# Means of the values: earlier loads on 128 partitions, a product on TensorE that adds halves, and value tiles of two blocks

## Chip, cores and metric

One program on one core of a Trainium2 chip. The metric is the device time of one execution in microseconds (us). The engines are TensorE (PE; PEld is its weight load), VectorE (DVE), ScalarE (ACT), GpSimd (POOL) and SyncE (SP, which here only issues DMAs and loads registers). The core has 16 DMA engines, which all queues share.

## The reference, cut to what matters

```python
B, H, S, D = 4, 8, 768, 64;  block, window = 32, 16
k_sum = k.reshape(B, H, 24, 32, D).max(axis=3)
v_sum = v.reshape(B, H, 24, 32, D).mean(axis=3)
scores = concat([where(|i - j| < 16, q @ k.T / 8, -1e9), q @ k_sum.T / 8 + log(32)])
attn   = softmax(scores) @ concat([v, v_sum])
x      = attn as [B * S, H * D]                       # 3072 tokens of 512
e      = argmax(x @ w_gate)                           # one of 8 experts a token
out    = gate * sigmoid(x @ w_output_gate)[e] * (relu(x @ w1[e]) @ w2[e])
```

Attention is local (a band of 16 on each side) with 24 summaries a head: the largest key and the mean value of each 32 tokens. A mixture of experts with one expert a token follows. The change is in how the 24 mean values of each head are made and brought to where the attention product reads them.

## The kernel before

**Stages.** A batch has 768 tokens, which are 6 "tokens tiles" (`tok`) of 128, or 12 blocks of 64. A stage is `(b, tok, g)`: 128 queries and 4 of the 8 heads; there are 48 stages. For a stage, `scores(i)` multiplies queries by the 96 keys of the band and the 24 summaries (120 columns a block; tile `sp`), DVE adds the mask and takes the minimum (`sm`, `mn`), ACT takes the exponential (`pr`), `turn_p(i)` transposes it on TensorE (`pt`, evacuated to `pT`), and `values(i)` multiplies it by the 120 rows of values of that block (`pv`), after which DVE divides (`xs`) and POOL stores 128 tokens to `x_dr`. `scores` is written one stage ahead of `turn_p`, and `values` one behind. `turn_x`, `logits`, `turn_logits` and `route` compute the gates some stages later; the last batch also carries the first expert's weights (`late_work`). The expert products (`hp`, `yp`) follow.

**Loads.** Queries and keys come in thirds of a batch (`raw_q`, `raw_k`), are reordered by a copy (`nat_q`, `nat_k`, mostly on DVE) and transposed (`qtr`, `ktr`). Queries of a third are loaded two thirds ahead, at an even `tok`, and reordered at the next `tok`.

**Values.** `VW` is a ring of 9 tiles of one block each: 120 partitions of 8 heads by 72 columns (64 values, a one, padding). Rows 0 to 47 and 72 to 119 are the band, loaded by `load_vw` in two DMAs a block with runs of 256 bytes; rows 48 to 71 are the 24 means, loaded by `load_vsum` from the DRAM tensor `vs_dr` in runs of 256 bytes, for 9 of a batch's 12 blocks (the other three find a tile of the same batch that has them). The means themselves: `load_vm` brings 4 heads of a batch's values as 96 partitions (4 heads by 24 summaries) of 32 rows; `v_sum` halves them five times on POOL (32 rows to 1), `mean` scales, and a POOL DMA stores 96 rows of 256 bytes to `vs_dr`. The first half of batch 0 is reduced by DVE instead. For batch b + 1 this happens during stages 1 to 7 of batch b.

**What sets the order.** SP's instructions stand as the code writes them; the other engines' order (but POOL's and parts of DVE's in the expert part) is set by a scheduler at build time, which keeps each engine's queue fixed: an instruction that waits holds up all that stand behind it on its engine. So a value load that waits for a ring tile to come free also holds up the query and key loads behind it on SP. SP's loads for token tile `tok + 2` are written at stage `(tok, 0)`.

Of the kernel before, what the change touches and what calls it, by code (L numbers as in the profile page):

```python
# [15 lines left out]
ALU = mybir.AluOpType  # L16
# [15 lines left out]
BUFS = {"sm": 4, "mn": 4, "pr": 4, "pT": 3, "xs": 3, "den": 3, "xT": 2, "ls": 2, "rawk": 3, "rawq": 2, "natk": 2, "natq": 2}  # L32
RAWS = 6
RAWS2 = 10
VR = 9
# [37 lines left out]
C_END = C_SEL + 2 * E  # L73


def constants():
# [22 lines left out]
    c[:, C_SEL:C_SEL + 2 * E] = p[:, None] % 32 == np.arange(2 * E)[None, :]  # L99
    return c  # L100
# [77 lines left out]
def attention(tc, const, sa, sb, st, ps, dr, q, k, v, id_sb, c_sb, wg_sb, x_dr, l_dr, rt, late_work):  # L178
# [24 lines left out]
    vs_dr = dr.tile([B, H, NS, D], F32, name="vs_dr")  # L203
# [21 lines left out]
    def load_vm(b, *os):  # L225
        for o in os:
            t = sa.tile([96, 32 * D], F32, name=f"vm{b}{o}", tag="vm", bufs=2)
            nc.sync.dma_start(t, v[b, 4 * o:4 * o + 4].rearrange("g (n s) d -> (g n) (s d)", n=NS))
            vm[b, o] = t

    vs = {}

    def v_sum(b, o, half):
        t = vm[b, o]
        if (b, o) == (0, 0):
            if half == 0:
                vs[b, o] = sb.tile([96, D], F32, name=f"vs{b}{o}", tag="vs", bufs=2)
            hs = slice(32 * half, 32 * half + 32)
            i = nc.vector.tensor_reduce(out=vs[b, o][:, hs], in_=t.rearrange("p (s d) -> p d s", d=D)[:, hs, :], axis=AX.X,
                                        op=ALU.add)  # L240

            tc.add_manual_dep(i.ins, km["last"].name, mybir.DependencyInfo(mybir.DependencyClass.NoSync,
                                                                           mybir.DependencyReason.SCHED_ONLY))
            if half == 1:
                mean(b, o, vs[b, o])
            return

        n = 16 * D
        if half == 0:
            nc.gpsimd.tensor_tensor(t[:, 0:n], t[:, 0:n], t[:, n:2 * n], ALU.add)  # L250
            return
        while n > D:
            n //= 2
            nc.gpsimd.tensor_tensor(t[:, 0:n], t[:, 0:n], t[:, n:2 * n], ALU.add)
        mean(b, o, t[:, 0:D])

    def mean(b, o, total):
        r2 = sb.tile([96, D], F32, name=f"vm2{b}{o}", tag="vs2", bufs=2)
        if b == 0 and o == 0:
            nc.scalar.activation(r2, total, AF.Copy, scale=1.0 / 32.0)  # L260
        else:
            (nc.gpsimd if b == 0 else nc.vector).tensor_scalar(r2, total, 1.0 / 32.0, None, ALU.mult)
        nc.gpsimd.dma_start(vs_dr[b, 4 * o:4 * o + 4].rearrange("g n d -> (g n) d"), r2)

    def load_vw(b, tok):
        for blk in (2 * tok, 2 * tok + 1):
            t = VW[(NB * b + blk) % VR]
# [6 lines left out]
    def load_vsum(b, tok):  # L274

        for blk in (2 * tok, 2 * tok + 1):
            if blk < VR:
                nc.sync.dma_start(VW[(NB * b + blk) % VR][LW:LW + NS, :, 0:D], vs_dr[b].rearrange("h n d -> n h d"))
# [29 lines left out]
    def k_sum(b):  # L308
        kt = KT[b % 2]
        for hp in range(HP):  # L310
            own = kt[:, hp, PAD:PAD + NB * KW].rearrange("p (i w) -> p i w", w=KW)[:, :, 32:56]
            i = nc.vector.tensor_copy(own, km[b, 0][:, hp, :].unsqueeze(1).to_broadcast([P, NB, NS]))
        km["last"] = i.ins
# [15 lines left out]
    def scores(i):  # L329
# [4 lines left out]
        for x in range(2):  # L334
            for y in range(2):
                li = 2 * tt + y
                blk = 4 * u + li
                nc.tensor.matmul(sp[:, 2 * x + y, 0:W], lhsT=qt[:, 2 * g + x, li, :],  # L338
# [12 lines left out]
    def turn_p(i):  # L351
# [3 lines left out]
        for c in range(4):  # L355
            nc.tensor.transpose(pt[:, c, :], pr[:, c, :], id_sb)  # L356
# [700 lines left out]
```

## Time and profile before

| | |
|---|---|
| Three runs | 539.55, 544.69 (median), 546.93 us |
| Profiled execution | 537.39 us, of which the span of instructions is 535.6 us |
| Granted TensorE clock, mean | 0.978 |
| Busy: PE, PEld, DVE, ACT, POOL | 492.9, 428.5, 387.0, 336.2, 204.1 us |
| First and last `values` product | at 31.46 us and about 195 us |
| DMA | 117.98 MB in 117052 packets, 53787 of them under 512 bytes |

All that follows reads the profiled execution. Its times are microseconds from the span's start. In a timeline row the columns are start, duration, engine, line, operation, tile written <- tiles read, shape and count; what stands in brackets is the idle time of that engine ahead of the row, and what ended it. SPq is SP's DMA queue. In a windows row the columns are the window, its length, busy time (and count) of PE, PEld, DVE, ACT and POOL, the granted TensorE clock, the mean busy share of the 16 DMA engines (it can pass 1 where packets of several queues overlap) and GB/s.

### The profile page before, as it was taken

Reading aid. Unit: us, or ns where it says so; the run is one execution under the profiler, and the core shown is the slowest. Engines: PE = TensorE matmul, PEld = TensorE weight load, DVE = VectorE, ACT = ScalarE, POOL = GpSimd, SP = SyncE. Lnnn points to the kernel's source line nnn. Section 1 sums busy time; section 2 is a strip of 40 time slices with the busy share of each in tenths; the row PEclk is TensorE's granted clock in tenths of the full one; section 3 lists DMA queues with packets and bytes.
Section 4 is the critical chain, followed back from the end, with each engine's and each line's share of the span. In section 5 each row is a group of like instructions: output and inputs, shape, how many; then the busy total and the mean of one; then the engine's idle time right before and its main releaser. Section 6 shows DMA issues by size and latency. Waiting matters only on the chain.

```text
span 535.6 us, 12274 instructions
## 1 busy us (share of the span) xinstructions
PE 492.9 (92%) x3880; PEld 428.5 (80%) x3880; DVE 387.0 (72%) x1238; ACT 336.2 (63%) x753; POOL 204.1 (38%) x231
## 2 busy tenths in 40 slices
PE   5899998789987999999999999999999999999990
PEld 5687887587766798789898998989897887987870
DVE  8877888479958868987666667675667767768660
ACT  4776786487769756554655656565567567558460
POOL 7527157245443432333735071421333421611321
PEclk9789999899999999999999999999999999999996
DMA  8989999899698577595966749486476796696640
GB/s 246 242 207 249 231 247 207 178 222 263 157 196 226 167 236 253 190 193 183 331 205 218 230 166 319 143 284 214 183 264 204 258 304 237 216 311 241 198 159 30
DMA packets 117052, 117.98 MB, mean 220 GB/s; under 512 B 53787, under 2 KB 78651, under 8 KB 116192
## 3 DMA queue, kind: packets, MB, share of 16 engines
q1 hardware_dynamic: 107584, 97.02, 64.5%
q0 software_dynamic: 9376, 19.91, 11.3%
q8 instruction: 36, 0.59, 0.5%
q14 instruction: 56, 0.46, 0.3%
HBM read 106.30 MB, written 13.79 MB: 224 GB/s over the span
## 4 chain that ended last, share of the span: by engine, by line
PE 61%; DMA 17%; DVE 6%; SPq 5%; issue 4%; ACT 3%; POOL 0%; POOLq 0%; ACTq 0%; DVEq 0%
PE hp L846 8%; PE hp L845 8%; PE hp L847 8%; PE yp L945 7%; PE yp L943 7%; PE yp L944 7%; DMA xg<-x_dr,lst_w 5%; PE sp L338 4%; DMA raw_q<-in_q_dram 4%; DMA vw<-vs_dr 3%; PE pv L367 3%; DMA raw_k<-in_k_dram 2%; PE pt L356 2%; PE xp L827 2%; SPq L272 1%
## 5 line engine op out<-in xcount | busy, mean ns | idle before, releaser
L845 PE MATMUL hp<-xhl,w1h 128*128 128x256 f32 x384 | 108.4, 284 | 1.1 <-ACT w2h L815 1.1
L846 PE MATMUL hp<-xhl,w1h 128*128 128x256 f32 x384 | 108.8, 284 | 0.0
L847 PE MATMUL hp<-xhl,w1l 128*128 128x256 f32 x384 | 108.5, 283 | 0.1
L943 PE MATMUL yp<-w2h,hh 128*128 128x512 f32 x216 | 86.5, 401 | 0.3 <-ACT hh L914 0.2
L945 PE MATMUL yp<-w2h,hl 128*128 128x512 f32 x216 | 84.9, 395 | 0.1
L944 PE MATMUL yp<-w2l,hh 128*128 128x512 f32 x216 | 84.9, 393 | 0.0
L794 POOL DMA_INDIRECT xg<-x_dr,lst_w x26 | 30.5, 1173 | 123.5 <-PE xp L827 118.7
L845 PEld LDWEIGHTS hp<-xhl,w1h 128*128 128x128 f32 x384 | 73.2, 191 | 2.9 <-issue 1.5
L846 PEld LDWEIGHTS hp<-xhl,w1h 128*128 128x128 f32 x384 | 73.5, 191 | 2.1 <-DVE xhl L830 0.9
L847 PEld LDWEIGHTS hp<-xhl,w1l 128*128 128x128 f32 x384 | 73.5, 191 | 0.3 <-issue 0.3
L348 ACT ACTIVATE pr<-sm,mn 128x120 f32<-128x120 f32 x192 | 61.5, 386 | 18.3 <-DVE mn L346 17.9
L848 ACT ACTIVATE hh<-hp 128x256 fp32r<-128x256 f32 x96 | 35.2, 380 | 53.4 <-PE hp L847 43.6
L849 DVE SCALAR_TENSOR_TENSOR hl<-hp,hh 128x256 fp32r<-128x256 f32 x96 | 38.8, 419 | 37.6 <-ACT hh L848 22.9
L338 PE MATMUL sp<-kt,qt 128*128 128x120 f32 x384 | 53.6, 287 | 2.2 <-DVE mn L346 0.8
L338 PEld LDWEIGHTS sp<-kt,qt 128*128 128x128 f32 x384 | 48.4, 199 | 5.6 <-issue 2.3
L945 PEld LDWEIGHTS yp<-w2h,hl 128*128 128x128 f32 x216 | 40.4, 188 | 9.8 <-DVE hl L915 1.2
L346 DVE CUSTOM_DVE_ANT_0 sm<-sp,c_sb 128x120 f32<-128x120 f32 x192 | 42.2, 276 | 8.2 <-PE sp L338 5.3
L943 PEld LDWEIGHTS yp<-w2h,hh 128*128 128x128 f32 x216 | 40.7, 188 | 8.6 <-ACT hh L914 0.7
L944 PEld LDWEIGHTS yp<-w2l,hh 128*128 128x128 f32 x216 | 40.7, 188 | 7.9
L356 PE MATMUL pt<-id_sb,pr 128*120 128x128 f32 x192 | 38.7, 288 | 4.6 <-ACT pr L348 1.9
L367 PE MATMUL pv<-vw,pT 120*64 120x65 f32 x768 | 36.3, 231 | 6.8 <-DVE xs L377 2.8
L367 PEld LDWEIGHTS pv<-vw,pT 120*64 120x64 f32 x768 | 28.6, 139 | 16.0 <-issue 7.9
(736 smaller groups left out, 1039.5 us busy)
## 6 DMA issues: line engine op xcount, KB each, us to landing
vw<-in_v_dram SPq DMA_DIRECT2D x88, 96.0 KB
raw_k<-in_k_dram SPq DMA_DIRECT2D x12, 512.0 KB
raw_q<-in_q_dram SPq DMA_DIRECT2D x12, 512.0 KB
vm<-in_v_dram SPq DMA_DIRECT2D x8, 768.0 KB
x_dr<-xs POOLq DMA_DIRECT2D x24, 256.0 KB
vw<-vs_dr SPq DMA_DIRECT2D x36, 48.0 KB
vw<-in_v_dram SPq DMA_DIRECT2D x8, 64.0 KB
xg<-x_dr,lst_w POOLq DMA_INDIRECT x26
```

The costliest lines, as they stand in the source:

```text
L338: nc.tensor.matmul(sp[:, 2 * x + y, 0:W], lhsT=qt[:, 2 * g + x, li, :], rhs=kt[:, 2 * g + x, blk * KW:blk * KW + W], start=True, stop=True)
L346: nc.vector.tensor_tensor_reduce(out=sm[:, c, :], in0=sp[:, c, 0:W], in1=c_sb[:, m:m + W], scale=1.0, scalar=3.0e38, op0=ALU.add, op1=ALU. ...
L348: nc.scalar.activation(pr[:, c, :], sm[:, c, :], AF.Exp, bias=mn[:, c:c + 1], scale=-1.0)
L356: nc.tensor.transpose(pt[:, c, :], pr[:, c, :], id_sb)
L367: nc.tensor.matmul(po[64 * y:64 * y + 64, 2 * x + hh, :], lhsT=pT[:, 2 * x + y, 64 * hh:64 * hh + 64], rhs=VW[(NB * b + 2 * tok + y) % VR] ...
L845: nc.tensor.matmul(hp, lhsT=w_h[:, fs], rhs=self.xh[:, c, :], start=c == 0, stop=False)
L846: nc.tensor.matmul(hp, lhsT=w_h[:, fs], rhs=self.xl[:, c, :], start=False, stop=False)
L847: nc.tensor.matmul(hp, lhsT=w_l[:, fs], rhs=self.xh[:, c, :], start=False, stop=c == NC - 1)
L849: nc.vector.scalar_tensor_tensor(hl[:, j, :], hp, 0.0, hh[:, j, :].bitcast(F32), ALU.max, ALU.subtract)
L943: nc.tensor.matmul(y, lhsT=hh[:, j, tk], rhs=w_h, start=j == 0, stop=False)
L944: nc.tensor.matmul(y, lhsT=hh[:, j, tk], rhs=w_l, start=False, stop=False)
L945: nc.tensor.matmul(y, lhsT=hl[:, j, tk], rhs=w_h, start=False, stop=j == NF - 1)
```

## The change

- **Loads of values for the means** (`load_vm`): three a batch instead of two, each 256 tokens of all 8 heads on 128 partitions (head, 16 tokens) of 16 rows; 4 buffers of 4 KB a partition instead of 2 of 8 KB. From batch 2 on they are issued during the batch before the previous one (`load_ahead`).
- **Sums** (`v_sum`): POOL halves three times (16 rows to 2), in one stage; none for batch 0, and none on DVE.
- **A product** (`v_mean`): TensorE multiplies by a constant of 128 by 64 (`C_MEAN`, 1/32 where head and summary agree), adding up the 2 rows that are left (16 rows for batch 0) and the two partitions of a summary, into 64 rows (8 summaries by 8 heads); ACT copies it to one of three tiles `mean0` to `mean2`, which carry the one and the padding.
- **The store** (`v_store`) writes 64 rows of 288 bytes; `vs_dr` now is [batch, summary, head, 72], so that `load_vsum` reads 2304 bytes in one piece a summary.
- **The ring** has 5 tiles of two blocks (10 blocks) instead of 9 of one. `load_vsum` fills both blocks with one DMA, for 5 of 6 token tiles, and stands one stage later in SP's order. Of the ring's memsets only the ones and 32 rows of one block are left.
- **`natq`** has one buffer instead of two.

```diff
-BUFS = {..., "natk": 2, "natq": 2}
+BUFS = {..., "natk": 2, "natq": 1}
-VR = 9
+VR = 5
...
+    for h, s in np.ndindex(H, 8):
+        c[16 * h + 2 * s:16 * h + 2 * s + 2, C_MEAN + 8 * s + h] = 1.0 / 32.0
...
-        t = sb.tile([W, H, VP], F32, name=f"vw{i}", tag=f"vw{i}", bufs=1)
-        nc.gpsimd.memset(t, 0.0)
-        nc.gpsimd.memset(t[:, :, D:D + 1], 1.0)
+        t = sb.tile([W, 2, H, VP], F32, name=f"vw{i}", tag=f"vw{i}", bufs=1)
+        if i == 0:
+            nc.gpsimd.memset(t[0:32, 0], 0.0)
+        nc.gpsimd.memset(t[:, :, :, D:D + 1], 1.0)
...
+    def load_vm(b, o):
+        t = sa.tile([P, 16 * D], F32, name=f"vm{b}{o}", tag="vm", bufs=4)
+        nc.sync.dma_start(t, v[b, :, 256 * o:256 * o + 256].rearrange("h (x s) d -> h x (s d)", s=16))
+        vm[b, o] = t
+    def v_sum(b, o):
+        t, n = vm[b, o], 16 * D
+        while n > 2 * D:
+            n //= 2
+            nc.gpsimd.tensor_tensor(t[:, 0:n], t[:, 0:n], t[:, n:2 * n], ALU.add)
+    def v_mean(b, o, after=None):
+        t = vm.pop((b, o))
+        mt = ps.tile([64, D], F32, name=f"mt{b}{o}", tag="TR", bufs=PB["TR"])
+        rows = 16 if b == 0 else 2
+        for s in range(rows):
+            i = nc.tensor.matmul(mt, lhsT=c_sb[:, C_MEAN:C_MEAN + 64], rhs=t[:, s * D:(s + 1) * D], start=s == 0,
+                                 stop=s == rows - 1)
+            ...
+        evac("mt", means[o][:, 0:D], mt)
+    def v_store(b, o):
+        nc.gpsimd.dma_start(vs_dr[b, 8 * o:8 * o + 8].rearrange("n h d -> (n h) d"), means[o])
...
+        if tok < VR:
+            t = VW[(TB * b + tok) % VR][LW:LW + NS]
+            nc.sync.dma_start(t.rearrange("n y h d -> n y (h d)"),
+                              vs_dr[b].rearrange("n h d -> n (h d)").unsqueeze(1).to_broadcast([NS, 2, H * VP]))
...
     def load_ahead(b, tok):
+        if tok in (0, 2) and b + 1 < B:
+            load("k", k, b + 1, 1 + tok // 2)
+        if tok == 4 and b + 2 < B:
+            load("k", k, b + 2, 0)
+        if tok in (2, 3, 5) and b + 2 < B:
+            load_vm(b + 2, (2, 3, 5).index(tok))
...
-        if more and u < 2 and s in (1, 3):
-            second.append(lambda: v_sum(b + 1, u, s // 2))
+        if more and i % 12 < 7:
+            o, what = divmod(i % 12, 2)
+            if o < 3:
+                second.append(lambda: (v_mean if what else v_sum)(b + 1, o))
+            if what == 0 and o > 0:
+                second.append(lambda: v_store(b + 1, o - 1))
```

Where this moves instructions. **TensorE at the start**: the stages of batch 0, token tiles 0 to 2 (names end in batch, token tile, g; `mt02` is batch 0, third 2). Before:

```order
L338 MATMUL sp000_306<-kt0_143,qt0_141 128x120 x4
L338 MATMUL sp001_328<-kt0_143,qt0_141 128x120 x4
L356 MATMUL pt000_351<-id_sb_66,pr000_313 120x128
L338 MATMUL sp010_367<-kt0_143,qt0_141 128x120 x4
L356 MATMUL pt000_351<-id_sb_66,pr000_313 120x128 x3
L338 MATMUL sp011_424<-kt0_143,qt0_141 128x120 x4
L356 MATMUL pt001_383<-id_sb_66,pr001_335 120x128 x3
L289 MATMUL qtr010_344<-id_sb_66,nat_q01_290 128x128 x4
```

and now the same place on TensorE:

```order
L339 MATMUL sp000_281<-kt0_143,qt0_141 128x120 x4
L255 MATMUL mt00_297<-vm00_180,c_sb_68 64x64 x16
L255 MATMUL mt01_316<-vm01_182,c_sb_68 64x64 x16
L339 MATMUL sp001_341<-kt0_143,qt0_141 128x120 x4
L358 MATMUL pt000_364<-id_sb_66,pr000_288 120x128 x4
L339 MATMUL sp010_409<-kt0_143,qt0_141 128x120 x4
L291 MATMUL qtr010_357<-id_sb_66,nat_q01_271 128x128 x4
L255 MATMUL mt02_371<-vm02_184,c_sb_68 64x64 x16
```

Two groups of 16 mean products stand between the first two stages' scores, and the third group behind the transposes of the second third's queries, `qtr010`. (TensorE's first `values` product, `pv000`, now stands behind the scores of seven stages; before it stood behind five.)

**SP in batch 1**: around the loads of the queries `raw_q21` and keys `raw_k30`, which the code writes at token tile 4 of batch 1. Before:

```order
L271 DMA vw4_163<-in_v_dram 48x8x64
L272 DMA vw4_163<-in_v_dram 48x8x64
L271 DMA vw5_166<-in_v_dram 48x8x64
L272 DMA vw5_166<-in_v_dram 32x8x64
L209 DMA raw_q21_1480<-in_q_dram 128x8x128
L209 DMA raw_k30_1482<-in_k_dram 128x8x128
L271 DMA vw6_169<-in_v_dram 32x8x64
L272 DMA vw6_169<-in_v_dram 48x8x64
```

and now the same place on SP:

```order
L239 DMA vm31_1387<-in_v_dram 128x1x1024
L272 DMA vw1_154<-in_v_dram 48x8x64
L273 DMA vw1_154<-in_v_dram 48x8x64
L272 DMA vw1_154<-in_v_dram 48x8x64
L273 DMA vw1_154<-in_v_dram 32x8x64
L221 DMA raw_q21_1534<-in_q_dram 128x8x128
L221 DMA raw_k30_1536<-in_k_dram 128x8x128
L272 DMA vw2_156<-in_v_dram 32x8x64
```

The order of the loads is much the same; what differs is when a ring tile is free. The load ahead of `raw_q21` fetches block 11 of batch 1. In the ring of 9 its tile `vw5` was last read for block 2 of that batch (token tile 1); in the ring of 5 pairs its tile `vw1` was last read for token tile 0, one token tile (two stages) earlier. The first expert products and all that follows them on each engine stand as before.

More of the change, by code (lines that the diff above doesn't have):

```diff
@@ L72 @@
 C_SEL = C_PART + 1
-C_END = C_SEL + 2 * E
+C_MEAN = C_SEL + 2 * E
+C_END = C_MEAN + 64
 def constants():
@@ L201, in evac @@
             nc.scalar.activation(dst, src, AF.Copy, scale=1.0 if scale is None else scale)
-    vs_dr = dr.tile([B, H, NS, D], F32, name="vs_dr")
+    vs_dr = dr.tile([B, NS, H, VP], F32, name="vs_dr")
+    means = []
+    for i in range(3):
+        t = sb.tile([64, VP], F32, name=f"mean{i}", tag=f"mean{i}", bufs=1)
+        nc.vector.memset(t[:, D:VP], 0.0)
+        nc.vector.memset(t[:, D:D + 1], 1.0)
+        means.append(t)
     raws, nat = {}, {}
@@ L349, in scores @@
         prs[i] = pr
+        return i_sp
     def turn_p(i):
@@ L478, in attention @@
     load("q", q, 0, 0)
-    load_vm(0, 0, 1)
+    for o in range(3):
+        load_vm(0, o)
     for u in range(3):
@@ L519, in attention @@
     n = len(stages)
-    scores(0)
+    i_sp = scores(0)
+    for o in range(2):
+        v_mean(0, o, i_sp)
+        v_store(0, o)
     for i, (b, tok, g) in enumerate(stages):
@@ L561, in attention @@
             work()
-        turn_p(i)
+        i_pt = turn_p(i)
+        if i == 0:
+            v_mean(0, 2, i_pt)
+            v_store(0, 2)
+            for t in range(3):
+                load_vsum(0, t)
+            for x in range(1, 3):
+                load_vm(1, x)
         second = first[1:] + second
```

76 lines of the change are left out of this document (18 added, 58 removed).

## Prediction, made before the run

> **What bounds the kernel now.** I read the page's head and chain first, then the busy times by stretch, then the waits of the stretch that is worst.
>
> ```profile
> span 535.6 us, 12274 instructions
> PE 61%; DMA 17%; DVE 6%; SPq 5%; issue 4%; ACT 3%; POOL 0%; POOLq 0%; ACTq 0%; DVEq 0%
> ```
>
> TensorE carries 61% of the chain; DMA follows with 17%. The stretches differ, though:
>
> ```profile
> 16.30:31.46 15.16, 13.77 (x76) 11.59 (x77) 10.64 (x46) 10.99 (x31) 6.93 (x8) 0.76 0.88 173
> 31.46:82.00 50.54, 49.11 (x600) 42.69 (x600) 41.52 (x222) 39.77 (x108) 22.52 (x27) 1.00 1.08 247
> 82.00:120.00 38.00, 30.52 (x337) 25.35 (x335) 25.97 (x132) 24.04 (x66) 19.93 (x22) 0.96 0.97 202
> 120.00:150.00 30.00, 27.97 (x337) 22.81 (x335) 26.99 (x153) 20.46 (x54) 14.56 (x17) 1.00 0.88 207
> 150.00:205.00 55.00, 49.05 (x537) 42.25 (x538) 42.16 (x200) 41.45 (x102) 22.04 (x25) 1.00 0.74 199
> 205.00:535.60 330.60, 312.54 (x1925) 275.01 (x1923) 225.61 (x468) 191.47 (x378) 108.37 (x99) 0.98 0.68 223
> ```
>
> From 205 us on the experts' products fill TensorE (312.5 of 330.6 us), and the change moves nothing there. What it can touch are the 189 us between the first scores (16.30) and 205. In 31.46 to 82 TensorE is busy for 49.1 of 50.5 us: nothing that only frees DMA or DVE can gain much there. From 82 to 120 it is busy for 30.5 of 38 us, and to 205 it idles another 8 us. The DMA share is near 1 up to 120 us, but it is a mean of 16 engines, with holes in it. The deepest stall shows how they arise:
>
> ```profile
> 91.01 0.40 SPq L209 DMA_DIRECT2D raw_q<-in_q_dram  x1
> ...
> 100.53 0.69 DVE L220 COPY nat_q<-raw_q 128x1024 f32<-128x1024 f32 x1 [3.61 <-DMA raw_q<-in_q_dram]
> ...
> 102.28 1.14 PE L367 MATMUL pv<-vw,pT 120*64 120x65 f32 x16 [2.80 <-DVE xs L377]
> ...
> 92.00:94.00 2.00, 2.00 (x30) 1.77 (x29) 1.19 (x12) 2.00 (x8) 1.53 (x2) 1.00 0.31 45
> 102.00:104.00 2.00, 1.72 (x24) 1.15 (x24) 0.89 (x3) 0.00 (x0) 1.18 (x2) 0.56 0.50 84
> ```
>
> SP issues the queries' load only at 91.01, with the DMA engines near idle (share 0.31 in 92 to 94); they land 9.5 us later, DVE stands before its copy for 3.61 us, and the division `xs` behind that copy keeps TensorE's product waiting for 2.80 us. The granted clock then falls to 0.56. SP was late because loads into the ring (L271) wait for products that free its tiles:
>
> ```profile
> SPq L271 <- PE pt L356: 7.5, 6, 3.7
> SPq L278 <- DMA vs_dr<-vm: 5.9, 2, 3.3
> ```
>
> **The change part by part.**
>
> *Products for the means.* No such product is in the trace. A call of an f32 product leaves two records, a transpose one. Prices per call from the chain:
>
> ```profile
> 65.52 0.62 PE pv L367 x16
> 62.87 1.78 PE sp L338 x16
> 54.57 0.58 PE pt L356 x4
> ```
>
> A `values` call (64 columns of weights, 65 moving) costs 0.62/8 = 0.078 us, a `scores` call (128 and 120) 1.78/8 = 0.22 us. The new call (64 and 64) is nearest to `values`; but there neighbours go to alternating halves of the columns, and here all add up in one place, so I take twice that, 0.155 us, with 0.078 and 0.22 as ends. Batches 1 to 3 have 18 calls: 18 x 0.155 = **+2.8 us** (1.4 to 4.0) on a TensorE that is nearly full. Batch 0 has 48: 7.4 us (3.7 to 10.6).
>
> *Start.* What lies there now:
>
> ```profile
> L338 PE MATMUL sp<-kt,qt 128*128 128x120 f32 x40 | 7.6, 357 | 1.1 <-ACT qt L201 0.6 <-issue 0.5
> L356 PE MATMUL pt<-id_sb,pr 128*120 128x128 f32 x20 | 4.8, 311 | 0.8 <-ACT pr L348 0.8
> L289 PE MATMUL qtr<-id_sb,nat_q 128*128 128x128 f32 x8 | 1.7, 354 | 0.0
> L289 PE MATMUL ktr<-id_sb,nat_k 128*128 128x128 f32 x8 | 1.7, 354 | 0.0
> ...
> 15.95 3.70 DVE L239 TENSOR_REDUCE vs<-vm 96x32 f32<-96x1024 f32 x2
> 21.95 1.17 DVE L220 COPY nat_q<-raw_q 128x1024 f32<-128x1024 f32 x1 [0.69 <-DMA raw_q<-in_q_dram]
> 25.42 0.57 POOL L263 DMA_DIRECT2D vs_dr<-vm  x1 [0.30 <-POOL vm L262]
> 27.99 2.48 SPq L278 DMA_DIRECT2D vw<-vs_dr  x6
> 31.46 0.45 PE L367 MATMUL pv<-vw,pT 120*64 120x65 f32 x4
> ```
>
> From 16.30 to 31.46 TensorE needs 40 x 0.11 + 20 x 0.145 + 16 x 0.145 = 9.6 us at the pace above, so at most 5.6 of the 15.2 us are free; at the clock of 0.76 granted there, the same work takes 12.6 us and only 2.6 are free. That cover hides part of the 7.4 us: +1.8 to +4.8. DVE's 3.70 us of sums go, so the first masks can start earlier; but the first transposes now stand behind 32 mean products on TensorE, which eats that gain. The chain to the first `values` product stays as long: the third group of mean products stands behind `qtr010`, which needs the queries copied at 21.95 to 23.1; with its 2.5 us, ACT's copy, 0.57 us for the store and 2 us of landing (25.99 to 27.99 before) the means can be loaded at about 29, against 27.99. Gained in return: SP has three loads of 512 KB ahead of the means' loads, so the engines no longer run dry around 28 us. The two `scores` moved ahead of the first `values` only change places. I take **+3 us**, with ends of -2 (all mean products hidden, first product as early as the loads allow) and +7.
>
> *Ring and queue.* The ring of ten blocks frees each tile a token tile earlier; 48 stages from 31.46 to about 195 make 3.4 us a stage, so loads behind it can go up to 6.8 us earlier, more than the 3.61 us DVE waited at 100.53. Loads of means no longer stand in SP's queue right behind a store (5.9 us waited in two pieces). The stalls in TensorE that follow from late loads are these:
>
> ```profile
> PE pv L367 <- DMA vw<-vs_dr: 2.0, 3, 1.1
> ...
> 155.84 0.66 PE L387 MATMUL xtr<-id_sb,xs 128*128 128x128 f32 x4 [1.28 <-DVE lg L197]
> ```
>
> Sum: 2.80 at 102.28, 2.0 for means, 1.28 at 155.84 (on DVE's copy of `lg`, itself behind a copy of late queries), and 0.9 for the slow clock (2 us at 0.56): 7.0 us. I take **-7.0**, with 0 and -13 as ends (the second is worked out below). What is late next is TensorE's own work.
>
> *GpSimd and copies.*
>
> ```profile
> L250 POOL TENSOR_TENSOR vm<-vm 96x1024 f32<-96x1024 f32 x7 | 16.5, 2359 | 32.5 <-DMA vm<-in_v_dram 22.3 <-DVE xs L377 10.2
> L254 POOL TENSOR_TENSOR vm<-vm 96x512 f32<-96x512 f32 (+3 forms) x28 | 20.7, 744 | 1.5
> L220 DVE COPY nat_k<-raw_k 128x1024 f32<-128x1024 f32 x11 | 10.8, 983 | 4.0 <-DMA raw_k<-in_k_dram 3.0 <-PE ktr L289 0.6 <-issue 0.2
> L220 DVE COPY nat_q<-raw_q 128x1024 f32<-128x1024 f32 x11 | 9.0, 822 | 13.0 <-DMA raw_q<-in_q_dram 13.0
> ```
>
> POOL's sums take 16.5 + 20.7 = 37 us now, for 7 loads of 1984 added elements a partition; 9 loads of 896 make 0.58 of that, 22 us. Off the path; but DVE's copies take 0.98 and 0.82 us in the mean where an undisturbed one takes 0.69 (row at 100.53): 11 x 0.29 + 11 x 0.13 = 4.6 us at most, if POOL's work were the whole reason. I take **-1** (0 to -4.6). DVE's six small scalings become nine on ACT, which idles enough.
>
> *One buffer for `nat_q`.* DVE's copy now waits until TensorE has transposed the third before, which stands a stage earlier. Behind it on DVE stand masks and divisions. No row shows such a wait; I take **+1** (0 to +3: eleven copies at the 0.27 us that a single transpose record lasts).
>
> Sum: 2.8 + 3 - 7.0 - 1 + 1 = **-1.2 us**. The profiled execution took 537.39 us (span 535.6 and 1.8 around it), so it would take 536.2. The runs' median, 544.69, lies 7.3 us above that execution; the difference applied to the median gives **543.5 us**.
>
> **The rivals.**
>
> *Slower: the value loads for the means run on half of the DMA engines.* Their source now is [8 heads][16][1024], where it was 96 rows. The weights' stretch, 300 to 400 us, gives a DMA engine's rate, and 28 to 33 us that of 256-byte pieces:
>
> ```profile
> q1 hardware_dynamic: 10441, 19.02, 55.2%
> q1 hardware_dynamic: 1269, 0.66, 55.8%
> ```
>
> 19.02 MB in 0.552 x 1600 us is 21.5 GB/s an engine. 512 KB take 1.5 us on 16 engines and 3.0 on 8: 12 loads add 18.3 us to the eight. The means' loads take back: their 36 DMAs of 192 pieces of 35 ns (0.558 x 80 us over 1269) are 15.1 us over 16 engines, and 20 new ones of 48 pieces of 2304 bytes at that rate 6.4, so 8.7 less. With +9.6 on the loads, and +3 and +2.8 on TensorE, nothing gained: 560 us. It decides where loads and not TensorE end last throughout; the full TensorE of 31 to 82 us beside a DMA share of 1.08 speaks against. Chance 0.11. The Trainium skill, DMA: Bandwidth & Descriptors, section "Why a DMA increments its semaphore by 16 and not by 1", says that a DMA is spread over the largest number of engines up to 16 that divides the outermost dimension of both its sides; by that rule these loads get 8 engines, as this rival has it. The trace before has no load of that shape.
>
> *Faster: the stretches after 82 us run as full as the one before.* (30.5 + 28.0 + 49.1)/0.97 = 110.9 against 123 us, and 0.9 for the clock, is -13.0; with 2.8 for the later products, the start free and -1: 533.5 us. The DVE-heavy last batch (42 of 55 us, with the weights' split) speaks against. Chance 0.17.
>
> *Only the wait moves.* The queries' own two raw buffers, or the engines' fixed order, hold SP back just as long: +3 + 2.8 - 1 + 1 gives 550.5 us. Chance 0.17.
>
> **How the numbers follow.** The forecast has 0.55, and by itself spans 537 to 549. A range of 530 to 555 takes in the faster and the unmoved case, each with some 4 us for the spread of the runs shown (539.55 to 546.93), and leaves out the slower one and tails. 2% of the median, about what a measurement of this kernel can tell from no change, is 10.9 us. Faster by more: most of the second rival's chance, 0.16; slower by more: 0.10; the rest, 0.74, within.
>
> **What would show it.** The start: the first `values` product at 33 to 36 us. The ring: SP's waits for TensorE's transposes at the `vw` loads (7.5 us above) falling below 4, DVE's wait for `raw_q` (13.0 us in the row above) to under 5, no clock below 0.9 after 40 us. The products: 16 calls (32 records) of batch 0 taking about 2.5 us. Wrong it would be if the mean products wait for their loads or for POOL's sums, with `values` behind them on TensorE, or if a load for the means takes over twice as long as one of `raw_k`, and `raw_q` is later than before.

## Result and profile after: slower by 6.4%

| | before | after |
|---|---|---|
| Median of 4 runs | 542.15 us (539.55 to 546.93) | **579.21 us** (574.39 to 583.28) |
| Ratio of the timed rounds, 95% interval | 1 | **1.064** (1.052 to 1.077) |
| Profiled execution, span | 537.39, 535.6 us | 579.0, 577.2 us |
| Granted TensorE clock, mean | 0.978 | 0.95 |
| First and last `values` product | 31.5 and 195.1 us | 44.0 and 231.9 us |

The ratio leaves out the run of 583.28 us, which was in a slower state than the others. The forecast was 543.5 us with a range of 530 to 555, a gain of 1.2 us: it had the wrong sign of the effect. The head and chain of the page after:

```profile
span 577.2 us, 12557 instructions
PE 53%; DMA 23%; DVE 8%; SPq 5%; issue 5%; ACT 3%; POOL 1%; POOLq 0%; DVEq 0%; ACTq 0%
```

DMA's share of the chain has grown from 17% to 23%, TensorE's fell from 61% to 53%. By the same stretches as before:

```profile
31.46:82.00 50.54, 39.05 (x403) 32.88 (x403) 29.14 (x139) 27.11 (x74) 18.30 (x26) 0.86 0.89 211
82.00:120.00 38.00, 35.90 (x438) 30.60 (x437) 32.22 (x167) 28.99 (x83) 16.89 (x22) 1.00 0.86 205
120.00:150.00 30.00, 17.57 (x153) 14.79 (x154) 12.60 (x62) 13.14 (x36) 5.13 (x7) 0.77 0.82 175
150.00:205.00 55.00, 45.65 (x491) 38.38 (x491) 39.65 (x227) 37.38 (x100) 17.58 (x21) 0.91 0.71 154
```

From 31.46 to 82, where TensorE had been busy for 49.1 us, it is busy for 39.05, and the granted clock is 0.86. From 120 to 150 it idles 12.4 of 30 us. What it waits for shows in the waits, here of SP's queue and of DVE and TensorE:

```profile
SPq L279 <- DMA vs_dr<-mean: 26.5, 3, 12.0
SPq L272 <- PE pt L358: 19.2, 6, 6.5
...
DVE nat_k L232 <- DMA raw_k<-in_k_dram: 20.1, 6, 11.1
DVE nat_q L232 <- DMA raw_q<-in_q_dram: 9.6, 2, 6.9
PE sp L339 <- DVE kt L314: 10.8, 1, 10.8
PE mt L255 <- POOL vm L247: 5.3, 2, 3.5
```

Two things are new. SP stands 26.5 us in three pieces at loads of means (L279), for the store of those means; it was 5.9 us in two. And DVE waits 20.1 us for keys (`raw_k`), where it waited 3.0. The deepest stall joins them, in rows of POOL, PE, ACT and SP (the last row is of a window):

```profile
83.82 0.46 POOL L247 TENSOR_TENSOR vm<-vm 128x128 f32<-128x128 f32 x1
...
106.31 0.45 PE L255 MATMUL mt<-vm,c_sb 128*64 128x64 f32 x4
108.89 0.22 ACT L207 ACTIVATE mean<-mt 64x64 f32<-64x64 f32 x1
110.90 0.54 POOL L263 DMA_DIRECT2D vs_dr<-mean  x1
110.86 0.79 SPq L273 DMA_DIRECT2D vw<-in_v_dram  x1
118.77 0.30 SPq L279 DMA_DIRECT2D vw<-vs_dr  x1
125.17 4.27 SPq L221 DMA_DIRECT2D raw_k<-in_k_dram  x1
136.86 3.77 PE L339 MATMUL sp<-kt,qt 128*128 128x120 f32 x16 [10.80 <-DVE kt L314]
...
111.65:118.77 7.12, 7.12 (x104) 6.17 (x104) 5.66 (x24) 5.45 (x15) 5.17 (x6) 1.00 0.38 97
```

POOL's halvings of the third group of batch 2 end at 84.28 (the row at 83.82). Its product runs on TensorE only 22 us later, at 106.31, its copy at 108.89. POOL then finishes halvings of batch 3, which stand ahead in its order, and issues the store at 110.90. SP has issued its last load before the means' at 110.86 and then issues nothing until 118.77, when the store has landed. In those 7.12 us the DMA share is 0.38. The keys' load, written behind, goes out at 125.17 and lands 10.7 us later; DVE stands 11.1 us before its copy. By the order of the code these are keys of batch 3. What TensorE stands 10.80 us for is a copy into `kt` of batch 2 (L314), which stands behind the keys' copy on DVE. In the kernel before, the stores of the same means went out by 90.71, and their first load only at 101.25: POOL halved and stored on its own, ahead of the stages. Now the means pass through TensorE's queue, where `mt22` stands behind the scores of stage (1, 4, 0), and wait there for their turn.

The 26.5 us have two parts. In the three pieces SP is free at 30.4, 111.65 and 155.5; the stores go out at 31.48, 110.90 and 165.55, and SP goes on at 38.03, 118.77 and 167.66. So some 11 us pass before a store's issue (1 and 10 us of the first and third piece), and some 15 between issue and landing.

The start shows the same (timeline, then the groups of 16 to 34 us for the 48 mean products), and the groups of the span show the one gain, in DVE's copies:

```profile
18.49 5.21 PE L255 MATMUL mt<-vm,c_sb 128*64 128x64 f32 x64
27.80 2.08 PE L255 MATMUL mt<-vm,c_sb 128*64 128x64 f32 x32
31.48 0.53 POOL L263 DMA_DIRECT2D vs_dr<-mean  x1 [6.70 <-ACT mean L207]
38.03 1.15 SPq L279 DMA_DIRECT2D vw<-vs_dr  x3
38.95 0.69 PE L255 MATMUL mt<-vm,c_sb 128*64 128x64 f32 x4 [3.45 <-POOL vm L247]
44.02 1.69 PE L370 MATMUL pv<-vw,pT 120*64 120x65 f32 x32
...
L255 PE MATMUL mt<-vm,c_sb 128*64 128x64 f32 x96 | 7.3, 248 | 0.0
...
L232 DVE COPY nat_k<-raw_k 128x1024 f32<-128x1024 f32 x11 | 7.6, 693 | 20.2 <-DMA raw_k<-in_k_dram 20.1
```

In the chain that ended last, the keys' load follows a value load (start, duration, what):

```profile
28.19 7.72 DMA vm<-in_v_dram
39.27 7.18 DMA vm<-in_v_dram
46.47 11.83 DMA raw_k<-in_k_dram
```

Where the time went, by the start of a stage's first `scores` product (from TensorE's records, 8 a stage), before and as a lag of the kernel after and of three experiments told below:

| stage (counted from 0) | before, us | after | e1 | o1 | s3 |
|---|---|---|---|---|---|
| 1 (0, 0, 1) | 18.1 | +5.5 | +5.1 | +4.5 | +0.1 |
| 7 (0, 3, 1) | 35.0 | +10.6 | +4.6 | +5.8 | -0.6 |
| 13 (1, 0, 1) | 62.7 | +20.3 | +11.5 | +11.4 | +10.3 |
| 23 (1, 5, 1) | 91.1 | +20.5 | +10.5 | +13.3 | +8.1 |
| 27 (2, 1, 1) | 111.5 | +30.9 | +17.2 | +11.9 | +5.3 |
| 37 (3, 0, 1) | 152.4 | +29.5 | +15.8 | +10.5 | +4.1 |
| 41 (3, 2, 1) | 161.7 | +37.7 | +20.3 | +8.3 | +3.7 |
| 47 (3, 5, 1) | 184.6 | +36.3 | +18.9 | +9.0 | +4.7 |

The lag comes in four steps of some 10 us: at the start, from stage 7 to 13, and around two later batch boundaries (23 to 27, 37 to 41), each after a long stand of SP for means. Behind the last `values` product the kernel after takes 4.8 us more: 535.6 - 195.1 = 340.5 and 577.2 - 231.9 = 345.3 us. What follows explains the 36.8 us up to that product.

### The profile page after: what moved, and what is told of

Same layout as the page of the kernel before. It is cut to its first block, busy times and chain, and to the rows that moved or that the text cites. A ratio compares the mean times of both kernels' runs of the same rounds, so it can differ in the third digit from the quotient of the medians.

```text
span 577.2 us, 12557 instructions
## 1 busy us (share of the span) xinstructions
PE 509.0 (88%) x4012; PEld 442.7 (77%) x4012; DVE 384.1 (67%) x1236; ACT 338.1 (59%) x764; POOL 186.8 (32%) x214
## 3 DMA queue, kind: packets, MB, share of 16 engines
q0 software_dynamic: 9504, 19.96, 10.6%
## 4 chain that ended last, share of the span: by engine, by line
PE 53%; DMA 23%; DVE 8%; SPq 5%; issue 5%; ACT 3%; POOL 1%; POOLq 0%; DVEq 0%; ACTq 0%
PE hp L862 7%; PE hp L861 7%; PE hp L863 7%; PE yp L961 6%; PE yp L959 6%; PE yp L960 6%; DMA xg<-x_dr,lst_w 6%; DMA raw_k<-in_k_dram 5%; PE sp L339 4%; DMA vm<-in_v_dram 3%; PE pv L370 2%; DMA raw_q<-in_q_dram 2%; PE xp L843 2%; SPq L272 2%; DMA raw_('e', 0)_2_2703<-in_moe_w_dram 2%
## 5 line engine op out<-in xcount | busy, mean ns | idle before, releaser
L810 POOL DMA_INDIRECT xg<-x_dr,lst_w x26 | 30.4, 1171 | 125.1 <-PE xp L843 115.6
L339 PE MATMUL sp<-kt,qt 128*128 128x120 f32 x384 | 59.5, 307 | 11.4 <-DVE kt L314 10.8
L339 PEld LDWEIGHTS sp<-kt,qt 128*128 128x128 f32 x384 | 54.3, 219 | 16.9 <-DVE kt L314 11.8
L347 DVE CUSTOM_DVE_ANT_0 sm<-sp,c_sb 128x120 f32<-128x120 f32 x192 | 42.8, 278 | 19.6 <-PE sp L339 18.9
L370 PEld LDWEIGHTS pv<-vw,pT 120*64 120x64 f32 x768 | 28.3, 141 | 12.7 <-issue 4.2
```

The source lines that it names most:

```text
L339: i_sp = nc.tensor.matmul(sp[:, 2 * x + y, 0:W], lhsT=qt[:, 2 * g + x, li, :], rhs=kt[:, 2 * g + x, blk * KW:blk * KW + W], start=True, st ...
L347: nc.vector.tensor_tensor_reduce(out=sm[:, c, :], in0=sp[:, c, 0:W], in1=c_sb[:, m:m + W], scale=1.0, scalar=3.0e38, op0=ALU.add, op1=ALU. ...
L370: nc.tensor.matmul(po[64 * y:64 * y + 64, 2 * x + hh, :], lhsT=pT[:, 2 * x + y, 64 * hh:64 * hh + 64], rhs=VW[(TB * b + tok) % VR][:, y, 4 ...
```

## Experiments

Ratios are to the kernel before, run beside each group of experiments, with the 95% interval; its median there was 536.9 to 538.6 us. Theory A: the value loads for the means run on half of the DMA engines, and what queues behind them is late. Theory B: the number of engines does not matter, the order does, as the loads for the means stand a batch sooner in SP's queue, ahead of loads of keys and queries. Others get their letter where they appear. The stretches up to the last `values` product are read from one profiled execution of each kernel, so a difference of 1 or 2 us between them shows nothing by itself.

**Loads with an outermost dimension of 16 (e1), 8 (the change) and 4 (e3).** Only the order of dimensions of the load changes, with the constant's rows permuted to match (e1), or the load is cut in two of 4 heads (e3).

```diff
-  v[b, :, 256 * o:256 * o + 256].rearrange("h (x s) d -> h x (s d)", s=16)
+  v[b, :, 256 * o:256 * o + 256].rearrange("h (x s) d -> x h (s d)", s=16)    # e1
+  two loads: t[64 * y:64 * y + 64], v[b, 4 * y:4 * y + 4, ...]                # e3
```

> The changed kernel with one edit: the means' loads read their rows with the 16 row groups of a head outermost and the 8 heads inside (and the constant of the mean product permuted to match), where the changed kernel has the 8 heads outermost; same bytes, same 4096-byte pieces, every instruction in the same order. Theory A (the loads ran on 8 of 16 DMA engines, and all loads behind them waited for those eight): the time falls from 579 to what the prediction's sum gave, 535 to 550 us, the load of the second batch's first third lands in under 4 us where it took 7.72, the first values product starts before 38 us where it starts at 44.02, and DVE's and ACT's waits for raw_k fall from 26 us to under 10. Theory B (it is the order: three loads for the means a batch sooner stand ahead of the loads of keys and queries in SP's queue, on however many engines): 572 to 585 us, and the waits for raw_k stay above 20 us.

> The changed kernel with each load for the means cut in two loads of 4 heads each (12 more issues on SP, some 0.6 us each, half of them at idle times). Theory A, with the number of engines that of the outermost dimension (4): 512 KB on 4 engines are 6.1 us where 8 take 3.0, 37 us more on those four over 12 loads: 605 to 630 us. Theory A in a weaker form (the loads are slow for another reason than the number of engines, such as rows of one head lying together): 575 to 590 us. Theory B: 575 to 590 us.

Measured: e1 557.63 us, **1.040 (1.035 to 1.045)**; e3 588.42 us, **1.097 (1.089 to 1.105)**. With 1.064 for the change, the order is that of the outermost dimension, 16, 8, 4. The same load takes 5.09 us instead of 7.72, and the last `values` product comes 17.4 us earlier in e1 and 13.1 us later in e3 than at 231.9:

```profile
26.25 5.09 DMA vm<-in_v_dram
...
L370 PE MATMUL pv<-vw,pT x768: 222/222/370, 38.5 to 214.5; 120*64 120x65 f32 x192
```

```profile
L371 PE MATMUL pv<-vw,pT x768: 219/222/370, 53.8 to 245.0; 120*64 120x65 f32 x192
```

The times decide for neither theory. e1 lies between the ranges of A and B, and its signs fall short of A's (5.09 us where under 4 was said, the first `values` product at 38.5); e3 lies below A's range, in that of the weaker form and of B. What decides is in the packets. The pages' rows for SP's queue (packets, MB, share), first of the change, then of e1, have the same bytes and 96 packets more in e1:

```profile
q1 hardware_dynamic: 102176, 97.46, 59.6%
q1 hardware_dynamic: 102272, 97.46, 62.3%
```

In the traces the 96 are packets of 4 bytes, 8 for each of the 12 loads; e3, with 24 loads, has as many as the change. The loads' own packets, 4096 bytes each, are the same 1536 in all three and take 0.25 us in the mean in the change, 0.27 in e1 and 0.20 in e3. But at most 11 of them are under way at a time in the change, 19 in e1 and 7 in e3. This fits 8, 16 and 4 engines, each with a little overlap, and not slower packets as in the weaker form. So A holds for some 13 us by the ratios (1.064 - 1.040 of 540) and 17.4 by the traces, and it cannot be all: e1 is still 4.0% slower than before, and its waits for means are hardly shorter:

```profile
SPq L279 <- DMA vs_dr<-mean: 23.4, 3, 12.0
...
DVE nat_k L232 <- DMA raw_k<-in_k_dram: 16.5, 7, 7.4
```

**An outermost dimension of 8 alone, in the kernel before (e2).** Nothing but the order of the partitions of `vm` (and of the store) is changed, so that the outermost dimension is 8 where it was 96.

```diff
-  ....rearrange("g (n s) d -> (g n) (s d)", n=NS)
+  ....rearrange("g (n s) d -> (g n) (s d)", n=NS).rearrange("(c a) f -> a c f", a=8)
```

> The kernel before with one edit: the means' loads take their 96 rows in the order 8 x 12 (every eighth row together), so that the outermost dimension of their source is 8, where it was 96; the stores of the means are permuted alike (24 KB each, 8 outermost). Bytes, pieces of 8192 bytes and the order of instructions stay. Theory A: 8 loads of 768 KB on 8 engines at 21.5 GB/s are 4.5 us instead of 2.2, 18 us more on those eight, and the loads behind them come late as in the changed kernel: 558 to 580 us. Theory B: nothing else is changed, 537 to 547 us.

Measured: 551.37 us, **1.028 (1.021 to 1.034)**: 14 us, below A's interval but far from nothing. POOL's wait for its loads rises from 22.3 to 34.6 us, and the last `values` product comes at 207.8 instead of 195.1. The Trainium skill, "DMA: Bandwidth & Descriptors", section "Why a DMA increments its semaphore by 16 and not by 1", says that a DMA uses the largest number of engines up to 16 that divides the outermost dimension of both sides. The traces agree: at most 11 packets of these loads are under way at a time in e2 where the kernel before has 20, and e2 has 64 packets of 4 bytes fewer, 8 for each of its 8 loads. The stores of the means changed too (8 packets each instead of 16), and SP's waits for them rose from 5.9 to 10.3 us, so not all of the 14 us need be the loads'.

**What is left in e1.** Theory C: it is where the loads of means stand. At the start too much stands ahead of them, and later SP reaches them before TensorE has made the means. Theory D, told below, is B's claim again for what is left. f1 puts the loads of `vm10`, `raw_q` and `raw_k` behind the first three loads of means; f2 halves the second and third group of batch 0 on POOL, so that only 16 of 48 calls of TensorE stay and 4 are added; f4 writes the loads of means one token tile later, from `tok + 2` to `tok + 1`; f124 does all three.

```diff
-        elif (tok + 2 < TB or more) and (b, tok) != (0, 0):
-            load_vsum(*divmod(b * TB + tok + 2, TB))
+        elif (tok + 1 < TB or more) and b * TB + tok > 1:           # f4
+            load_vsum(*divmod(b * TB + tok + 1, TB))
```

> The kernel of e1_outer16 with one more edit: the three loads of 512 KB that stand ahead of the first three loads of means in SP's queue (the second batch's first third for the means, raw_q and raw_k) stand behind them. Theory C (what is left of the loss, 21 us, comes of where the means stand: at the start behind 1.5 MB of other loads, later because SP reaches a load of means before TensorE has made them and stands there with all loads behind it): the first values product starts at 33 to 36 us where e1_outer16 has 38.5, SP's gap before the first loads of means falls from 7.7 to under 5 us, and the ratio to the kernel before falls from 1.040 to 1.027 to 1.035. Theory D (what is left comes of the loads for the means standing a batch sooner, which crowd the DMA engines in the first 120 us; the start is made up later): the first product moves as well, but the ratio stays at 1.037 to 1.045.

> The kernel of e1_outer16 with one more edit: in the first batch two of the three groups are halved on GpSimd first (six TENSOR_TENSOR) and take 2 products each, not 16; 28 of 48 mean products of the start go. Theory C: e1_outer16 has TensorE busy for 15.16 of 15.16 us from 16.30 to 31.46, its mean products take 5.45 + 2.08 us there; 4.4 us of them go, and the third store, at 29.50, comes 1 to 4 us sooner; ratio 1.030 to 1.040. Theory D: 1.035 to 1.045. If GpSimd's halvings are late, the products wait for them and it is slower than e1_outer16.

> The kernel of e1_outer16 with one more edit: each load of means after the first three stands two stages later in SP's queue (behind the next token tile's loads of values). Theory C: SP waited 23.4 us in three pieces for stores of means there (7.7, 3.9 and 12.2 us); the first piece stays, the other two fall to under 4 us together, loads of queries and keys behind them come sooner, ratio 1.015 to 1.030. Theory D: the ratio stays at 1.035 to 1.045 though the waits fall.

> The three edits of f1_start_order, f2_pool_sums and f4_vsum_later together on the kernel of e1_outer16. Theory C: they add up, ratio 0.99 to 1.015, first values product at 31 to 34 us. Theory D: 1.03 to 1.045.

Measured: f1 564.57 us, **1.050 (1.045 to 1.056)**; f2 560.37, 1.035 (1.020 to 1.049), too wide to call; f4 552.48, **1.029 (1.021 to 1.038)**; f124 563.64, **1.049 (1.043 to 1.055)**. f1 is the instructive miss, outside both ranges. Its first `values` product comes at 33.7 us instead of 38.5, as early as C wanted, and yet it is slower: SP's waits for means rise to 28.9 us, and its last `values` product comes at 221.5 against 214.5. f124 misses both ranges too. Only f4 gains, with the ratio that C gave, but not by C's sign: SP's waits for means are 19.1 us where e1 had 23.4, and under 12 was said.

**Too many loads at once?** Theory D: loads of `vm` a batch and more ahead crowd out the keys. d1 is f4 with those loads later (token tile 5 of the batch before the previous one, and 0 and 1 of the previous). d2 is f4 with two `nat_q` buffers (and one `sm` fewer for the space), d3 is d1 with the same. d4 is d1 with the halvings, products and stores of means two stages later.

```diff
-        if tok in (2, 3, 5) and b + 2 < B:
-            load_vm(b + 2, (2, 3, 5).index(tok))
+        if tok == 5 and b + 2 < B:
+            load_vm(b + 2, 0)
+        if tok in (0, 1) and b > 0 and b + 1 < B:
+            load_vm(b + 1, 1 + tok)
```

> The kernel of f4_vsum_later (ratio 1.029) with one more edit: from the third batch on, the three loads for the means stand later in SP's queue, at token tiles 5 of the batch two ahead and 0 and 1 of the batch ahead, where they stand at 2, 3 and 5 of the batch two ahead; that is near the places that they have in the kernel before. Theory D (the loads a batch sooner stand ahead of the loads of keys and queries while the DMA engines are full): the load of raw_k that e1_outer16 and f4_vsum_later issue at 59.0 us comes at 53 to 56, the 13th values stage, at 60.0 before and 79.0 in f4_vsum_later, starts at 68 to 74, and the ratio is 1.005 to 1.022. Theory C (SP's and TensorE's order around the means): raw_k moves, the ratio stays at 1.024 to 1.036. Theory E (one nat_q buffer, the copies wait for TensorE): 1.024 to 1.036.

> The kernel of f4_vsum_later with nat_q in two buffers again, as before the change; for the space of it the masked scores (sm) have three buffers instead of four. Theory E: the copies of queries come a stage sooner, and the ratio falls from 1.029 to 1.005 to 1.02. Theories C and D: it stays at 1.024 to 1.036, or rises by under 0.5% for the buffer of sm.

> Both edits, of d1_late_loads and d2_natq2, on f4_vsum_later. Theory D: as d1_late_loads, 1.005 to 1.022. Theory E: as d2_natq2. If both count, 0.99 to 1.01.

> The kernel of d1_late_loads with the halvings, mean products and stores of each batch two stages later too (stages 2 to 8 of the batch ahead where they have 0 to 6), so that no mean product waits on TensorE for a load or a halving. Theory C: mean products stood in TensorE's order with values behind them (2.21 us idle ahead of one at 47.54 in e1_outer16); these waits go, but the stores come two stages later and SP waits longer for them: within 0.7% of d1_late_loads. Theory D: the same as d1_late_loads.

Measured: d1 551.96 us, **1.026 (1.018 to 1.034)**; d2 556.91, 1.036 (1.029 to 1.044); d3 555.17, 1.033 (1.026 to 1.041); d4 557.02, 1.033 (1.024 to 1.043). d1 does not differ from f4, nor d4 from d1, so D is not borne out: the load of keys goes out at 54.2 us, as D said, but the 13th `values` stage starts only at 78.4 (79.0 in f4; before it starts at 65.5, not at 60.0 as the expectation has it). Nothing speaks for one buffer of `nat_q` as the cause, since the kernels with two are no faster; but these also have one `sm` fewer, which could hide a small gain.

**Taking SP's wait away (o1) and the later products (o2).** Theory C is now split: C1 is SP's wait for later means, C2 the mean products in TensorE's order. In o1 all loads of means read batch 0's row of `vs_dr`; their number, size and place stay, and so do all products and stores. o2 drops the later products, halvings, copies and stores as well. Other means give other gates and so other lists of tokens for the experts: the time behind the last `values` product becomes 325.9 and 327.3 us instead of 341.1 in e1. So these two are read by that product, and not by the whole time.

```diff
-                              vs_dr[b].rearrange(...)
+                              vs_dr[0].rearrange(...)          # o1
-        if more and i % 12 < 7:
+        if False:                                              # o2, on top of o1
```

> The kernel of e1_outer16 with the loads of means of all batches reading the first batch's means: the later batches' means are made and stored but not used, so their values are wrong by that, and nothing in SP's queue waits for a store after the start. Theory C1 (what is left comes of SP waiting for means of later batches): SP's waits for stores of means fall from 23.4 to about 8 us, ratio from 1.040 to 1.015 to 1.025. Theory C2 (it comes of mean products standing in TensorE's order with values behind them, and of the start): the ratio stays above 1.03.

> The kernel of o1_means0 without the later batches' halvings, mean products, copies and stores (27 halvings, 18 product calls, 9 copies, 9 stores left out; their loads stay). What is left against the kernel before is then the start and the loads. Theory C2: the scores stages 8 to 13 (which lose 6 us in e1_outer16 after a 2.21 us wait of a mean product for its halving) lose nothing, and the ratio falls by 1 to 2% below o1_means0. Theory C1: as o1_means0, within 0.5%.

Measured: whole times 535.53 us, 0.998 (0.993 to 1.002), and 530.79, 0.989 (0.984 to 0.994). Waits and last products of o1, then the product of o2:

```profile
SPq L279 <- DMA vs_dr<-mean: 7.3, 1, 7.3
...
DVE nat_k L232 <- DMA raw_k<-in_k_dram: 8.1, 6, 2.9
...
L370 PE MATMUL pv<-vw,pT x768: 222/222/371, 39.5 to 204.6; 120*64 120x65 f32 x192
```

```profile
L370 PE MATMUL pv<-vw,pT x768: 219/222/371, 38.6 to 203.4; 120*64 120x65 f32 x192
```

Without the dependence on later means, SP waits once, at the start; DVE waits 8.1 us for keys instead of 16.5; and the last `values` product comes 9.9 us sooner than in e1. In the table of stages the steps of e1 at 23 to 27 and 37 to 41 are gone. The work of making the means itself is worth no more than about 1 us (204.6 against 203.4, one execution each). So C1 is shown: not the products cost, but that SP stands for their result. How much of it is the late store and how much its landing is not separated.

**Putting the loads of means as late as they may (h1, h2, s1, s2, s3).** h1 has e1 and d1's late loads, the loads of `vm11` and `vm12` ahead of the first loads of means, and the loads of means two stages later from batch 1 on; h2 is h1 with f2's sums. Theory S: what is left is the start, where TensorE carries the sums of batch 0. s1 is h1 with batch 0 halved on DVE (two groups) and POOL (one), so that 6 calls remain of 48; s2 has all three on DVE. s3 is s1 with later batches' loads of means one stage later again, at the very stage that reads them, and a plain rule for batch 0.

```diff
-            for j in (b * TB + tok + 1, b * TB + tok + 2): ...       # h1, s1: at g == 1
+            if b > 0:                                                # s3: at g == 0, behind load_vw
+                load_vsum(b, tok)
+        elif b == 0 and 0 < tok < 4:
+            load_vsum(0, tok + 2)
```

> The kernel of e1_outer16 with three edits: the second batch's second and third load for the means stand ahead of the first three loads of means in SP's queue (SP waits 7.7 us there for a store, the DMA share is 0.71 from 30 to 40 us); the loads of means stand two stages later from the second batch on (as in f4_vsum_later, but not in the first batch, where that made the seventh values stage wait for them until 62.5); the loads for the means stand later as in d1_late_loads. If TensorE's mean products of stages 3 and 5 waited for these two loads, the wait of 2.21 us at 47.54 goes, and the ratio falls to 1.005 to 1.02; if not, it stays at 1.02 to 1.03.

> The kernel of h1_ahead with the halvings of f2_pool_sums in the first batch (28 of 48 mean products of the start go, 4.4 us of TensorE). If the start's products still count once the later waits are gone: 1 to 4 us less than h1_ahead, ratio 0.995 to 1.015; if the loads set the pace there, the same as h1_ahead.

> The kernel of h1_ahead with the first batch's halvings made by VectorE (two groups) and GpSimd (one), so that all mean products of the start take 2 calls a group (6 of 48 calls stay). Theory S (the rest, some 8 us at the last values product, is the start: 32 mean products stand between the first and the second scores stage, which starts 5 us later than before): the second scores stage starts at 18 to 19 us where h1_ahead has 23.3, the first values product before 34, the last values product at 197 to 201 (before 195.1, h1_ahead 205.6), ratio 1.00 to 1.015. Theory T (the rest is made by loads that stand sooner, or by the engines' order later): the start moves, the ratio stays at 1.02 to 1.03.

> As s1_dve_sums, with all three groups of the first batch halved on VectorE. Theory S: within 0.5% of s1_dve_sums; VectorE's halvings stand ahead of masks, up to 1 us later masks.

> As s1_dve_sums, with each load of means of the later batches one stage later again in SP's queue (right behind the loads of values that stand two token tiles ahead, one stage before the values that read them). h1_ahead's SP still waited 6.7 and 6.1 us for stores of means at 93 and 142 us: if these still count, they fall to under 3 us each and the ratio is 1 to 2% below s1_dve_sums; if the means then land too late, TensorE waits for them and it is slower.

Measured: h1 549.03 us, **1.026 (1.020 to 1.031)**; h2 550.41, 1.026 (1.023 to 1.030); s1 551.43, 1.024 (1.016 to 1.032); s2 553.05, 1.029 (1.022 to 1.037); s3 543.93, **1.014 (1.006 to 1.022)**. Of s1 only the times are used. h2, s1 and s2 take most or all of the sums of batch 0 off TensorE and gain nothing, so S falls. The second `scores` stage does start as before (18.2 us in s3, 18.1 before), but the first `values` product only at 41.8, where S said before 34: what holds it up there is not those sums. Which of the loads ahead does is not shown. s3 gains 1% on s1 with the place of the loads alone changed, as was expected, though the two intervals overlap. SP's wait for means' stores is 23.4 us in e1, 16.6 in h1 and 4.6 in s3, and DVE's for keys 16.5, 11.2 and 5.9:

```profile
SPq L279 <- DMA vs_dr<-mean: 4.6, 2, 3.5
...
DVE nat_k L232 <- DMA raw_k<-in_k_dram: 5.9, 5, 3.0
...
L370 PE MATMUL pv<-vw,pT x768: 220/222/369, 41.8 to 197.4; 120*64 120x65 f32 x192
```

Its last `values` product comes 2.3 us later than before. s3 is the best version found that reads the right means, some 5% below the change; it does not beat the kernel before.

## Why the prediction was wrong

By the last `values` product the change costs 231.9 - 195.1 = 36.8 us. Of these 17.4 go with an outermost dimension of 16 (e1), 9.9 with SP's waits for later means (o1), about 1.2 with the later halvings and products (o2). The 8.3 left stand in o2 against before; s3 recovers most of them by order alone, though with another start, so how they split is not shown. Two steps of the prediction failed: a term with the wrong sign, and a cost put at nothing.

- **Ring and queue, -7.0: the step that failed in the sum.** It said that "Loads of means no longer stand in SP's queue right behind a store". They do: the waits went from 5.9 to 26.5 us, and o1 gets 9.9 us back by ending them after the start. Behind this lies a misread row. The 7.5 us of waits at the ring were taken as the reason that the queries' load went out only at 91.01. SP's rows of the kernel before show that the largest of them stands behind that load, not ahead of it:

```profile
87.58 0.73 SPq L271 DMA_DIRECT2D vw<-in_v_dram  x1
89.08 1.31 SPq L271 DMA_DIRECT2D vw<-in_v_dram  x1
91.45 1.72 SPq L209 DMA_DIRECT2D raw_k<-in_k_dram  x1
93.26 3.69 SPq L271 DMA_DIRECT2D vw<-in_v_dram  x1
```

The wait of 3.7 us is in the row at 93.26. From 80.39, the queries' load before, to 91.01 the ring's waits add up to 1.5 us, and from 82 to 90 the DMA share was 0.99 to 1.19. So an earlier free tile had little to give there. Two further facts were in hand and not joined. With tiles free sooner SP can come to the means' loads sooner; it came at 111.65, which less the stages' lag of 20.5 us is 91.2, where the kernel before had 101.25. And a mean now passes TensorE, ACT and POOL, of which TensorE is the engine that bounds: the product at 106.31 ran 22 us after its halvings. That the ring is what let SP run ahead is argued; no run has the old ring with the new means. The signs named ahead went against the term: SP's waits at the `vw` loads 19.2 us (7.5 before, "below 4" said), granted clock 0.86 from 31.46 to 82 and 0.77 from 120 to 150 (none below 0.9 after 40 said); DVE's wait for `raw_q` fell to 9.6 (13.0 before, "under 5" said), but the keys' rose from 3.0 to 20.1.
- **The loads for the means, put at nothing in the sum: the other step.** The slower rival, given 0.11 and 560 us, was real; e1, e2, e3 and their packets show it. Its gross price of 18.3 us for the loads is near what the last `values` product shows, 12.7 (e2, where the stores changed too) and 17.4 (e1). What was wrong is the argument against it, "the full TensorE of 31 to 82 us": full or not, TensorE stands when a copy on DVE waits for keys, and these queue behind the value loads (7.2 us, then 11.83 for `raw_k`). With the other step's reversal on top, the time passes that rival too.
- **Start, +3 (-2 to +7).** The first `values` product came at 44.0 us, where 33 to 36 was said; with the loads of e1 it came at 38.5, the upper end. The chain was followed up to the store's landing at 29, with 2 us for the landing; the third store went out at 31.48, and SP waited until 38.03. But the start did not set the end: f1 had 33.7 and was slower.
- **Products.** The price was right: 48 calls took 7.3 us (7.4 said), 16 calls 2.08 (2.5 said). The later ones were given 2.8; without them and their halvings o2's last product comes 1.2 us sooner. Two waits for POOL's halvings on TensorE (5.3 us) were named as what would make the prediction wrong, and they occurred.
- **GpSimd and copies, -1; `nat_q`, +1.** DVE's key copies did shorten, from 983 to 693 ns, those of queries from 822 to 726; together 4.2 us of DVE time that waited for loads instead. The second `nat_q` buffer brought nothing in d2, with one `sm` fewer.
- **The faster case** needed full stretches after 82 us; from 120 to 150 TensorE was busy for 17.6 of 30.

What stays open: why the store of 110.90 landed 7.9 us after its issue, and that of 165.55 only 2.1 us after (of 15 landings that the trace records for the first, 14 come by 114.39 and the last at 118.63; router stores follow it on POOL's queue, which was not tested); and why s3, whose last `values` product is 2.3 us late, takes 1.4% more in all: 344.2 us lie behind that product against 340.5.

## What to carry to other kernels

A load's first dimension matters even where its bytes and rows don't: in the kernel before, splitting 96 rows as 8 by 12, in loads and stores, cost 2.8%, and here "h x" against "x h" 2.4%. On an engine that only issues DMAs in order, a load that waits for a stored result stops every load behind it: put it at the last place its reader allows (s1 to s3: 1.024 to 1.014), above all after a change that lets the queue run ahead. And when work moves from an engine that runs ahead to the one that bounds, price not only its duration but how late its result will be, and who stands for it.

## What was not expected of the hardware

Keys and queries queued behind the loads pay: a 512 KB load of keys took 11.83 us in flight behind a value load of 7.18 us. And DVE's copies of 128x1024 took 983 ns in the mean beside POOL's long sums and 693 ns in the change, where POOL's busy time fell from 204 to 187 us; what of it is due to POOL was not separated.
